# Splitting and reordering the first loads, and a tile transposed by DMA instead of TensorE

## The chip, the cores and the metric

The kernel runs on one core of one Trainium2 chip. A core has a matmul engine (TensorE, PE in the profile), VectorE (DVE), ScalarE (ACT), GpSimd (POOL) and SyncE (SP), which run their own instruction lists and wait for each other by semaphores. SP and ACT can issue DMAs, each on a queue of its own; 16 DMA engines carry them. The metric is the device time of one execution in microseconds (us). Before the change it is 214.48 us, the median of 3 runs (214.37 to 214.8).

## The reference

From x (2048 x 512, bfloat16) it computes x + attention(layernorm(x)) + FFN(layernorm(x)).

```python
xn = _layernorm(x, axis=-1)
return x + _A_ref(xn, A_wqkv, A_wo) + _B_ref(xn, B_w_gate, B_w_up, B_w_down)
# _A_ref: linear attention, H = 32 heads of Dh = 16
phi = lambda t: jnp.where(t > 0, t + 1, jnp.exp(t)) + 1e-6
pq, pk = phi(q), phi(k)
kv = jnp.einsum("bhsd,bhse->bhde", pk, v)
z = jnp.einsum("bhsd->bhd", pk)
num = jnp.einsum("bhqd,bhde->bhqe", pq, kv)
den = jnp.einsum("bhqd,bhd->bhq", pq, z)[..., None] + 1e-6
# o = num / den, times wo
# _B_ref: (silu(x @ w_gate) * (x @ w_up)) @ w_down, F = 1792
```

## The kernel before

The 2048 rows of x are 16 tiles of 128 rows. Row p*16 + t of x is partition p of tile t, so a load of one tile moves 128 pieces of 1 KB, and a load of n tiles 128 pieces of n KB.

**Stage 1** goes over the tiles. For each tile, DVE computes the mean and variance (`bns` and `agg`, lines 273 and 276), POOL the reciprocal root (`rstd_pow`, lines 292 and 299), and DVE the normalized tile xn (line 281). xn is then transposed into xnT, since a projection needs the transpose as its stationary operand. Tiles 0 to 2 are transposed by PE against an identity matrix, and ACT copies the result out of PSUM (`transpose_half` for tile 0 in two halves, lines 336 and 345; `transpose_pe` for tiles 1 and 2, lines 308 and 315). From tile 3 on the DMA engines transpose, issued by SP (`transpose_dma`, line 352). PE projects K and Q of the tile, four matmuls each (`proj`, line 361; tile 0's K in two halves, line 374). ACT computes the exponentials of K and Q and a copy of Q (lines 397, 403, 407), DVE turns K into pk (`feat_k`: a clip at line 414 and a max-add at line 423). POOL adds pk up (line 448). PE then adds xn.T @ pk over all tiles in four PSUM banks, four matmuls per tile (`gtacc`, line 456, "GT" below). V is never projected: GT times wv gives the attention's kv later.

**Stage 2** is the FFN (line 548 for gate and up projections, in chunks of 512 rows) with the attention's small products between its matmuls, and the output tiles (lines 681 and 691), which DVE adds to x and SP stores.

What sets the order is the program text: each engine runs its instructions in the order in which the functions are called, and `_Prog` adds the semaphore waits. Around the change that is:
- Loads. SP issues x 0, the first half of wk, x 2, the first half of wq, then x 4-5 (which wait for x 0 and x 1 by the `after` list of `xload`), x 6-9, x 10-11 and x 12-15. ACT issues x 1, the second half of wk, x 3 and the second half of wq. Line 192 is the x load, line 199 the weight load.
- Idle matmuls. `fill` (line 244) multiplies a tile of zeros ahead of the first real work on PE: ten at once, one behind the variance of tile 0, one behind its reciprocal root, and one between tile 0's transposes and K.
- DVE's order at the start: stats 0, stats 1, xn 0 in halves, xn 1, stats 2, stats 3, xn 2, pk 0, xn 3.
- PE's order at the start: idle matmuls, transposes 0, K 0, transposes 1, Q 0, transposes 2, K 1, Q 1. In the loop over t (lines 505 to 531) K and Q of tile t follow for t >= 2, then GT of tile t - 2.
- SP has the x loads first in its list, then the transposes as they are called, then the FFN's weights (`wpiece` at line 210 in tiles 2, 4, 6 and 8, the rest from tile 11 on).

Of the kernel before, what the change touches and what calls it, by code (L numbers as in the profile page):

```python
# [10 lines left out]
P = 128  # L11
# [97 lines left out]
def bass_parallel_sum__linear_attn_block__swiglu_ffn__prompt_kernel(  # L109
# [12 lines left out]
    K = _Prog()  # L122
    pe, act, dve, pool, sp = nc.tensor, nc.scalar, nc.vector, nc.gpsimd, nc.sync
    bf, f32 = dt.bfloat16, dt.float32

    with contextlib.ExitStack() as es:
        E = es.enter_context

        def sb(name, shape, d=bf):
            return E(nc.sbuf_tensor(name, [P] + shape, d))  # L130

        x_sb = sb("x_sb", [NT, D])
# [11 lines left out]
        stats = sb("stats", [NT, 6], f32)  # L144
        mv = sb("mv", [NT, 2], f32)
        vpe = sb("vpe", [NT], f32)
        rstd = sb("rstd", [NT], f32)
# [35 lines left out]
        def bk(i):  # L183
            return ("bank", i)


        xv = xin.rearrange("(p t) d -> p t d", t=NT)
        ov = oview.rearrange("(p t) d -> p t d", t=NT)

        def xload(eng, h, t0, n, after=()):  # L190
            K.dma(
                eng, lambda: h.dma_start(x_sb[:, t0:t0 + n, :], xv[:, t0:t0 + n, :]),  # L192
                r=list(after), w=[("x", t0 + i) for i in range(n)],
            )

        def wqkv_load(eng, h, name, i, c0, n):
            K.dma(
                eng,
                lambda: h.dma_start(  # L199
                    wqkv_sb[:, c0:c0 + n, i * D:(i + 1) * D],  # L200
                    A_wqkv[c0 * P:(c0 + n) * P, i * D:(i + 1) * D].rearrange("(c p) f -> p c f", p=P),
                ),
                w=[(name, c0)],
            )
# [4 lines left out]
        def wpiece(name, dst, src, c):  # L209
            K.dma("sp", lambda: sp.dma_start(dst[:, c, :], src[c * P:(c + 1) * P, :]), w=[(name, c)])  # L210

        xload("sp", sp, 0, 1)
        xload("act", act, 1, 1)
        wqkv_load("sp", sp, "wk", 1, 0, 2)
        wqkv_load("act", act, "wk", 1, 2, 2)
        xload("sp", sp, 2, 1)
        xload("act", act, 3, 1)
        wqkv_load("sp", sp, "wq", 0, 0, 2)
        wqkv_load("act", act, "wq", 0, 2, 2)
        xload("sp", sp, 4, 2, [("x", 0), ("x", 1)])  # L220
        xload("sp", sp, 6, 4)
        xload("sp", sp, 10, 2)
        xload("sp", sp, 12, 4)

# [10 lines left out]
            r=[("ident",)], w=[("ident",)],  # L235
# [4 lines left out]
        def fill(n, after):  # L240
            K.op(
                "pe",
                [
                    (lambda: pe.matmul(banks[3], idle[:, 0:P], idle[:, :], start=True, stop=True))
                    for _ in range(n)
                ],
                r=[("idle",)] + after, w=[bk(3)],
            )
# [21 lines left out]


        def bns(t):
            K.op("dve", lambda: dve.bn_stats(stats[:, t, :], x_sb[:, t, :]), r=[("x", t)], w=[("st", t)])  # L273

        def agg(t):
            K.op("dve", lambda: dve.bn_aggr(mv[:, t, :], stats[:, t, :]), r=[("st", t)], w=[("mv", t)])

        def xn_dve(t):
            K.op(
                "dve",  # L280
                lambda: dve.tensor_scalar(
                    out=xn_sb[:, t, :], in0=x_sb[:, t, :], scalar1=mv[:, t, 0:1], scalar2=rstd[:, t:t + 1],
                    op0=ALU.subtract, op1=ALU.mult,
                ),
                r=[("x", t), ("mv", t), ("rstd", t)], w=[("xn", t)],
            )

        def rstd_pow(t):
            eng, h = ("dve", dve) if t == 0 else ("pool", pool)
            K.op(  # L290
                eng,
                lambda: h.tensor_scalar(
                    out=vpe[:, t:t + 1], in0=mv[:, t, 1:2], scalar1=1e-5, scalar2=None, op0=ALU.add,
                ),
                r=[("mv", t)], w=[("vpe", t)],
            )
            K.op(
                "pool",
                lambda: pool.tensor_tensor(out=rstd[:, t:t + 1], in0=vpe[:, t:t + 1], in1=nhalf[:, :], op=ALU.pow),
                r=[("vpe", t), ("nhalf",)], w=[("rstd", t)],  # L300
            )

        def transpose_pe(t, b):
            tb = banks[b].bitcast(bf)[:, 0:512].rearrange("p (c s) -> p c s", c=NDC)
            K.op(
                "pe",
                [
                    (lambda c=c: pe.transpose(tb[:, c, :], xn_sb[:, t, c * P:(c + 1) * P], ident[:, :]))  # L308
                    for c in range(NDC)
                ],  # L310
                r=[("xn", t), ("ident",)], w=[bk(b)],
            )
            K.op(
                "act",
                lambda: act.activation(xnT[:, :, t * P:(t + 1) * P], tb, ACT.Copy),
                r=[bk(b)], w=[("xnT", t)],
            )
# [31 lines left out]
        def transpose_dma(t):  # L349
            K.dma(  # L350
                "sp",
                lambda: sp.dma_start_transpose(out=xnT[:, :, t * P:(t + 1) * P], in_=xn_sb[:, t, :]),
                r=[("xn", t)], w=[("xnT", t)],
            )
# [15 lines left out]
        def proj_half(t, b, lo, wname, h):  # L370
            K.op(
                "pe",
                [
                    (lambda c=c: pe.matmul(
                        banks[b], xnT[:, c, t * P:(t + 1) * P], wqkv_sb[:, c, lo:lo + D],
                        start=(c == 0), stop=(c == NDC - 1),
                    ))
                    for c in (2 * h, 2 * h + 1)
                ],
                r=[("xnTh", t, h), (wname, 2 * h)], w=[bk(b)],  # L380
            )

        def kb(t):
            return 2 * (t % 2)
# [4 lines left out]
        def kproj(t):  # L389
            proj(t, kb(t), D, "wk")  # L390

        def qproj(t):
            proj(t, qb(t), 0, "wq")

        def exp_k(t):
            K.op(
                "act", lambda: act.activation(ek[:, t % NE, :], banks[kb(t)], ACT.Exp),  # L397
                r=[bk(kb(t))], w=[("ek", t % NE)],
            )
# [52 lines left out]
        def gtacc(t):  # L452
            K.op(
                "pe",
                [
                    (lambda c=c: pe.matmul(  # L456
                        banks[4 + c], xn_sb[:, t, c * P:(c + 1) * P], pkq[:, t, 0, :],
                        start=(t == 0), stop=(t == NT - 1),
                    ))
                    for c in range(NDC)  # L460
                ],
                r=[("xn", t), ("pk", t)], w=[bk(4 + c) for c in range(NDC)],
            )

        def stat(t):
            bns(t)
            agg(t)
            rstd_pow(t)

        def xn(t):  # L470
            xn_dve(t)
            if t >= 3:
                transpose_dma(t)

        stat(0)
        stat(1)
        xn_half(0, 0)
        xn_half(0, 1)
        xn_dve(1)
        stat(2)  # L480
        stat(3)
        xn_dve(2)

        fill(10, [])
        fill(1, [("mv", 0)])
        fill(1, [("rstd", 0)])
        transpose_half(0, 4, 0)
        transpose_half(0, 5, 1)
        fill(1, [])
        proj_half(0, kb(0), D, "wk", 0)  # L490
        proj_half(0, kb(0), D, "wk", 1)
        exp_k(0)
        transpose_pe(1, 6)
        qproj(0)
        exp_q(0)
        transpose_pe(2, 7)
        kproj(1)
        qproj(1)
        feat_k(0)
        xn(3)  # L500

        STAT = {0: (4, 5), 1: (6,), 2: (7,), 3: (8,), 4: (9, 10), 5: (11,), 6: (12,), 7: (13,), 8: (14, 15)}
        XN = {0: (4,), 1: (5,), 2: (6,), 3: (7,), 4: (8,), 5: (9, 10), 6: (11,), 7: (12,), 8: (13,), 9: (14, 15)}

        for t in range(NT):
            if t >= 2:
                kproj(t)
            if t >= 1:
                exp_k(t)
            if t >= 2:  # L510
                qproj(t)
            if t >= 1:
                exp_q(t)
                feat_k(t)
            for i in STAT.get(t, ()):
                stat(i)
            for i in XN.get(t, ()):
                xn(i)
            if t in (2, 4, 6, 8):
                wpiece("wg", wg_sb, B_w_gate, t // 2 - 1)  # L520
            if t == 11:
                for c in range(NDC):
                    wpiece("wu", wu_sb, B_w_up, c)
                wqkv_load("sp", sp, "wv", 2, 0, 4)
                wload("sp", sp, "wo", wo_sb, A_wo)
            if t == 14:
                wload("sp", sp, "wd", wd_sb, B_w_down)
            if t == 12:
                masks()
            if t >= 2:  # L530
                gtacc(t - 2)
        zsum(NT - 1, None)
        gtacc(NT - 2)
# [247 lines left out]
```

## Time and profile before

| what | us |
|---|---|
| median of 3 runs | 214.48 |
| the profiled execution | 215.03 |
| its span, first to last instruction | 213.8 |
| PE busy in the span | 208.2 (97%) |
| DVE, ACT, POOL busy | 117.9, 68.0, 70.1 |
| x 0 issued, statistics of tile 0 begin | 0.80, 3.94 |
| first transposes on PE | 6.34 |
| second half of wq issued on ACT, lands | 2.27, 9.36 |
| Q of tile 0 begins | 9.50 |
| first DMA transpose (tile 3) issued | 10.86 |
| first GT (tile 0) begins | 14.25 |

In a line of the timeline the columns are start, length (us), engine, line of the kernel, operation, the tile that is written and those that are read, shapes, and the count of instructions that were merged; in brackets stands the idle time before it and what ended it. SPq and ACTq are the queues' issuing instructions; PEld is PE's load of a stationary operand. Matmul ends are modelled (379 ns each); the distance from one to the next is their pace. In a line of DMA issues the last number is the time from issue to landing.

### The profile page before, as it was taken

How to read it: one execution, taken by the hardware profiler on the slowest of the kernel's cores; microseconds unless marked ns; L12 is line 12 of the kernel's file. 1: busy time of each engine (PE TensorE's matmuls, PEld its weight loads, DVE VectorE, ACT ScalarE, POOL GpSimd, SP SyncE). 2: the span in 40 equal slices, each digit the busy share in tenths (PEclk: the TensorE clock that was granted, in tenths of full speed). 3: DMA queues.
4: the chain of work that ended last, by engine and by line, in shares of the span. 5: the costliest groups of instructions: out<-in, count | busy, mean ns of one | idle time of the engine just before them, and what ended most of it. 6: DMA issues, size and time to landing. Idle time of an engine off the chain costs nothing.

```text
span 213.8 us, 2737 instructions
## 1 busy us (share of the span) xinstructions
PE 208.2 (97%) x974; PEld 96.2 (45%) x993; DVE 117.9 (55%) x239; ACT 68.0 (32%) x118; POOL 70.1 (33%) x93
## 2 busy tenths in 40 slices
PE   7799999999999999999999999999999999999996
PEld 2344444444544444444444444444444444444455
DVE  2899987333667777345463647365467364232121
ACT  2386666667463332213031303122132213121000
POOL 1559886647044444241212422141224140000000
PEclk9999999999999999999999999999999999999999
DMA  6925697898000111110111110101101102000001
GB/s 186 385 67 132 147 143 173 286 367 259 0 15 9 28 26 31 41 25 28 26 37 37 25 28 25 49 0 49 28 25 25 49 0 52 13 11 28 25 28 51
DMA packets 24495, 15.79 MB, mean 74 GB/s; under 512 B 16416, under 2 KB 22944, under 8 KB 24480
## 3 DMA queue, kind: packets, MB, share of 16 engines
q1 hardware_dynamic: 23648, 14.82, 26.6%
q10 hardware_dynamic: 832, 0.79, 1.1%
q8 instruction: 8, 0.13, 0.3%
q14 instruction: 7, 0.06, 0.1%
HBM read 9.70 MB, written 2.10 MB: 55 GB/s over the span
## 4 chain that ended last, share of the span: by engine, by line
PE 94%; DMA 3%; ACTq 1%; issue 1%; DVE 0%
PE psum L548 45%; PE psum L691 23%; PE psum L361 13%; PE psum L681 6%; PE psum L456 6%; DMA wqkv_sb<-in_A_wqkv_dram 3%; ACTq L192 0%; PE psum L607 0%; PE psum L630 0%; ACTq L199 0%; DVE out_sb L704 0%; PE psum L597 0%; PE psum L308 0%
## 5 line engine op out<-in xcount | busy, mean ns | idle before, releaser
L563 ACT ACTIVATE sg<-psum 128x512 bf16<-128x512 f32 x56 | 33.4, 598 | 105.4 <-PE psum L548 104.6
L548 PE MATMUL psum<-xnT,wg_sb 128*128 128x512 bf16 x224 | 57.5, 379 | 0.0
L548 PE MATMUL psum<-xnT,wu_sb 128*128 128x512 bf16 x215 | 56.7, 379 | 0.5
L639 POOL TENSOR_TENSOR prod<-pkq,zb 128x512 f32<-128x512 bf16 x16 | 18.6, 1162 | 51.5 <-DVE pkq L423 51.5
L548 PEld LDWEIGHTS psum<-xnT,wu_sb 128*128 128x128 bf16 x224 | 21.9, 98 | 26.4
L548 PEld LDWEIGHTS psum<-xnT,wg_sb 128*128 128x128 bf16 x224 | 21.9, 98 | 26.4
L704 DVE TENSOR_TENSOR out_sb<-psum,x_sb 128x512 bf16<-128x512 f32 (+1 forms) x17 | 11.2, 660 | 40.9 <-PE psum L691 40.9
L361 PE MATMUL psum<-wqkv_sb,xnT 128*128 128x512 bf16 x122 | 28.9, 379 | 1.3 <-DMA wqkv_sb<-in_A_wqkv_dram 1.1
L569 DVE TENSOR_TENSOR xn_sb<-psum,sg 128x512 bf16<-128x512 f32 x28 | 19.0, 680 | 18.7 <-PE psum L548 18.2
L663 POOL TENSOR_TENSOR pqn<-pkq,rden 128x512 bf16<-128x512 bf16 x16 | 16.9, 1055 | 36.6 <-DVE rden L657 36.6
L691 PE MATMUL psum<-wd_sb,xn_sb 128*128 128x512 bf16 (+1 forms) x124 | 25.6, 355 | 0.1
L691 PE MATMUL psum<-wd_sb,pkq 128*128 128x512 bf16 x109 | 25.3, 379 | 0.2
L569 DVE TENSOR_TENSOR pkq<-psum,sg 128x512 bf16<-128x512 f32 x28 | 18.8, 673 | 11.3 <-PE psum L548 8.5
L448 POOL TENSOR_TENSOR zacc<-zacc,pkq 128x512 f32<-128x512 f32 x15 | 17.3, 1154 | 6.9 <-DVE ek L414 6.7
L361 PEld LDWEIGHTS psum<-wqkv_sb,xnT 128*128 128x128 bf16 x124 | 11.9, 98 | 15.5 <-issue 1.3
L691 PEld LDWEIGHTS psum<-wd_sb,xn_sb 128*128 128x128 bf16 x126 | 12.2, 98 | 12.1 <-DVE xn_sb L569 0.5
L691 PEld LDWEIGHTS psum<-wd_sb,pkq 128*128 128x128 bf16 x112 | 11.0, 98 | 13.2
L681 PE MATMUL psum<-m_sb,eq 128*128 128x512 bf16 (+1 forms) x68 | 16.6, 366 | 0.0
L456 PE MATMUL psum<-pkq,xn_sb 128*128 128x512 bf16 x62 | 15.8, 379 | 0.1
L647 DVE TENSOR_REDUCE den<-prod 128x32 f32<-128x512 f32 x16 | 10.9, 683 | 5.8 <-POOL prod L639 5.8
L397 ACT ACTIVATE ek<-psum 128x512 bf16<-128x512 f32 x16 | 9.6, 599 | 9.9 <-issue 3.5
L273 DVE BATCH_NORM_STATS2 stats<-x_sb 128x6 f32<-128x512 bf16 x16 | 10.8, 678 | 2.8 <-DMA x_sb<-in_A_x_dram 2.8
(57 smaller groups left out, 126.3 us busy)
## 6 DMA issues: line engine op xcount, KB each, us to landing
out_dram<-out_sb SPq DMA_DIRECT2D x15, 128.0 KB, 1.7
wg_sb<-in_B_w_gate_dram SPq DMA_DIRECT2D x4, 448.0 KB, 4.2
wu_sb<-in_B_w_up_dram SPq DMA_DIRECT2D x4, 448.0 KB, 4.7
wd_sb<-in_B_w_down_dram SPq DMA_DIRECT2D x1, 1792.0 KB, 13.5
x_sb<-in_A_x_dram SPq DMA_DIRECT2D x2, 512.0 KB, 5.9
wqkv_sb<-in_A_wqkv_dram ACTq DMA_DIRECT2D x2, 256.0 KB, 5.7
wqkv_sb<-in_A_wqkv_dram SPq DMA_DIRECT2D x2, 256.0 KB, 4.7
x_sb<-in_A_x_dram SPq DMA_DIRECT2D x2, 256.0 KB, 5.1
```

Source lines behind the costliest of these rows:

```text
L361: (lambda c=c: pe.matmul(banks[b], xnT[:, c, t * P:(t + 1) * P], wqkv_sb[:, c, lo:lo + D], start=(c == 0), stop=(c == NDC - 1),))
L448: lambda: pool.tensor_tensor(out=zacc[:, :], in0=zacc[:, :], in1=pk, op=ALU.add),
L456: (lambda c=c: pe.matmul(banks[4 + c], xn_sb[:, t, c * P:(c + 1) * P], pkq[:, t, 0, :], start=(t == 0), stop=(t == NT - 1),))
L548: (lambda c=c: pe.matmul(banks[b], w_sb[:, c, fc * P:(fc + 1) * P], xnT[:, c, C * 512:(C + 1) * 512], start=(c == 0), stop=(c == NDC - 1),))
L563: lambda: act.activation(sg[:, j % NSG, :], banks[gb], ACT.Silu),
L569: lambda: dve.tensor_tensor(out=hT(C, fc), in0=banks[ub], in1=sg[:, j % NSG, :], op=ALU.mult,),
L639: lambda: pool.tensor_tensor(out=p, in0=pkq[:, t, 1, :], in1=zb[:, :], op=ALU.mult),
L647: lambda: dve.tensor_reduce(out=d, in_=p.rearrange("p (h e) -> p h e", e=DH), op=ALU.add, axis=AX.X,),
L663: lambda: pool.tensor_tensor(out=pqn[:, t % NPN, :].rearrange("p (h e) -> p h e", e=DH), in0=pkq[:, t, 1, :].rearrange("p (h e) -> p h e", ...
L681: (lambda g=g: pe.matmul(dst, pqnT(t)[:, g, :], m_sb[:, g, lo:hi], start=(g == 0), stop=False,))
L691: (lambda fc=fc: pe.matmul(dst, hT(C, fc)[:, jj * P:(jj + 1) * P], wd_sb[:, fc, lo:hi], start=False, stop=(fc == NFC - 1),))
L704: lambda: dve.tensor_tensor(out=o, in0=src, in1=x_sb[:, t, lo:hi], op=ALU.add),
```

## The change

x 0 is loaded in two parts of 64 rows, one on each queue. x 2 moves ahead of the weights on SP; x 3 moves from ACT to SP, behind wq; x 4-5 wait for both halves of wk, x 6-9 for both halves of wq, and x 10 to 15 follow. Tile 2 is transposed by DMA. DVE takes stats 2 ahead of xn 1 and stats 3 ahead of xn 2. On PE, three of the idle matmuls go, transposes 1 stand ahead of exp of K 0 in ACT's list too, and GT of tile 0 is called ahead of the loop, so that it comes before K of tile 2. In the loop, tiles 2 to 4 are followed by GT of tile t - 1, tile 5 by none, and later tiles by GT of tile t - 2 as before.

```diff
-        xload("sp", sp, 0, 1)
+        def xpart(eng, h, t, p0):
+            K.dma(
+                eng, lambda: h.dma_start(x_sb[p0:p0 + P // 2, t, :], xv[p0:p0 + P // 2, t, :]),
+                w=[("xp", t, p0)] + ([("x", t)] if p0 else []),
+            )
+
+        wk, wq = [("wk", 0), ("wk", 2)], [("wq", 0), ("wq", 2)]
+        xpart("sp", sp, 0, 0)
+        xpart("act", act, 0, P // 2)
         xload("act", act, 1, 1)
+        xload("sp", sp, 2, 1)
         wqkv_load("sp", sp, "wk", 1, 0, 2)
         wqkv_load("act", act, "wk", 1, 2, 2)
-        xload("sp", sp, 2, 1)
-        xload("act", act, 3, 1)
         wqkv_load("sp", sp, "wq", 0, 0, 2)
         wqkv_load("act", act, "wq", 0, 2, 2)
-        xload("sp", sp, 4, 2, [("x", 0), ("x", 1)])
-        xload("sp", sp, 6, 4)
+        xload("sp", sp, 3, 1)
+        xload("sp", sp, 4, 2, wk)
+        xload("sp", sp, 6, 4, wq)
         xload("sp", sp, 10, 2)
         xload("sp", sp, 12, 4)
...
         def bns(t):
-            K.op("dve", lambda: dve.bn_stats(stats[:, t, :], x_sb[:, t, :]), r=[("x", t)], w=[("st", t)])
+            K.op("dve", lambda: dve.bn_stats(stats[:, t, :], x_sb[:, t, :]),
+                 r=[("x", t)] + ([("xp", t, 0)] if t == 0 else []), w=[("st", t)])
...
         def xn(t):
             xn_dve(t)
-            if t >= 3:
+            if t >= 2:
                 transpose_dma(t)
...
         xn_half(0, 0)
         xn_half(0, 1)
-        xn_dve(1)
         stat(2)
+        xn(1)
         stat(3)
-        xn_dve(2)
+        xn(2)
 
         fill(10, [])
-        fill(1, [("mv", 0)])
-        fill(1, [("rstd", 0)])
         transpose_half(0, 4, 0)
         transpose_half(0, 5, 1)
-        fill(1, [])
         proj_half(0, kb(0), D, "wk", 0)
         proj_half(0, kb(0), D, "wk", 1)
+        transpose_pe(1, 6)
         exp_k(0)
-        transpose_pe(1, 6)
         qproj(0)
         exp_q(0)
-        transpose_pe(2, 7)
         kproj(1)
         qproj(1)
         feat_k(0)
         xn(3)
-
+        gtacc(0)
+
+        SKIP = 5
...
-            if t >= 2:
+            if 2 <= t < SKIP:
+                gtacc(t - 1)
+            elif t > SKIP:
                 gtacc(t - 2)
```

## The prediction

> **What bounds the kernel now.** I first read the busy shares, then the chain that ended last, then the first 18 us in order of time, and last how long single DMAs take to land. From the page:
>
> ```profile
> span 213.8 us, 2737 instructions
> ...
> PE 208.2 (97%) x974; PEld 96.2 (45%) x993; DVE 117.9 (55%) x239; ACT 68.0 (32%) x118; POOL 70.1 (33%) x93
> ...
> PE 94%; DMA 3%; ACTq 1%; issue 1%; DVE 0%
> ```
>
> PE is the engine that sets the end; the one other thing in the chain is 3% of DMA. The chain in order of time says where it lies (start, length, what):
>
> ```profile
> 2.27 7.09 DMA wqkv_sb<-in_A_wqkv_dram
> 9.50 1.02 PE psum L361 x4
> 10.75 3.45 PE psum L361 x16
> 14.25 0.81 PE psum L456 x3
> 15.06 1.73 PE psum L361 x8
> ```
>
> The second half of wq, issued on ACT's queue at 2.27, lands at 9.36, Q of tile 0 waits for it, and from 9.50 PE runs without a hole worth naming to the end. At 15.11 (14.25 and four matmuls of 0.216) it has done K and Q of tiles 0, 1, 2 and GT of tile 0. After the change the same work lies behind it when Q of tile 2 ends, since GT of tile 0 now comes ahead of K of tile 2. So the whole question is **when Q of tile 2 ends: before 15.11 is a gain, after it a loss**, one for one, if nothing stalls later. The rows that the new start hangs on, from the timeline:
>
> ```profile
> 1.25 5.25 PE L244 MATMUL psum<-idle 128*128 128x512 bf16 x12 [1.25 <-DVE idle L238]
> ...
> 3.94 0.69 DVE L273 BATCH_NORM_STATS2 stats<-x_sb 128x6 f32<-128x512 bf16 x1 [2.75 <-DMA x_sb<-in_A_x_dram]
> ...
> 4.18 1.91 SPq L192 DMA_DIRECT2D x_sb<-in_A_x_dram  x4
> ...
> 9.18 0.41 DVE L281 TENSOR_SCALAR xn_sb<-x_sb,mv,rstd 128x512 bf16<-128x512 bf16 x1 [0.20 <-POOL rstd L299]
> ...
> 10.86 7.62 SPq L352 DMA_TRANSPOSE xnT<-xn_sb  x4
> ```
>
> The reader sees: the idle matmuls begin at 1.25 on an otherwise empty PE, x 0 sets when DVE begins, xn 2 is written at 9.18, and SP issues x 4 to 15 already at 4.18 to 6.09, long before the first DMA transpose at 10.86, so the transposes never meet the x loads. And from the DMA view, single issues (KB, us to landing): the transpose issued at 17.30, the first piece of w_gate at 18.53, and the transpose behind that piece on SP's queue at 19.46:
>
> ```profile
> xnT<-xn_sb SPq DMA_TRANSPOSE x1, 2.4
> ...
> wg_sb<-in_B_w_gate_dram SPq DMA_DIRECT2D x1, 448.0 KB, 3.8
> ...
> xnT<-xn_sb SPq DMA_TRANSPOSE x1, 3.4
> ```
>
> A transpose with nothing ahead of it takes 2.4 us, one with a load ahead of it on SP's queue lands 0.59 us after that load (22.89 against 22.30). A queue serves in order.
>
> **The change, part by part.**
>
> Ten idle matmuls instead of thirteen. The three that go are 0.43, 0.43 and 0.22 us on PE. The ten end at 1.25 + 10 x 0.427 = 5.52, and PE idles until xn of tile 0 is there. Fills are 0.43 apart until 6.1, K of tile 0 is 0.22 apart from 7.09, though the granted clock reads 1.00 throughout: PE doubles its pace at about 6.3. If the hole of some 0.4 us at 5.5 keeps the pace low for a few us more, the two halves of K 0, four transposes and about three matmuls of Q 0 cost 0.86 + 0.2 + 0.65 = 1.7 us more. I cost it at nothing: the wait for tile 2 (below) covers it. The page "TensorE: Matmul & The Clock Gate" of the Trainium skill (section "What's actually happening") says that the pace follows how busy PE has lately been, and that about 3.4 us of busy time release it, so by it a thinner warm-up is a risk and not a saving. Put into the sum, its bad case moves the end of GT 0 from 11.4 to about 12.9, still short of the landing found below, and the time stays.
>
> x 0 in two halves. Both queues start with 64 rows; one more DMA issue, of 0.3 to 0.4 us, lands on each queue's front. x 0 landed at 3.92 (0.80 + 3.1) with x 1 beside it at 4.10. Bounds: nothing, to 0.5 us earlier; I take 0.2, so x 0 at 3.7; the first transposes on PE stand at 6.34 now. The chain DVE (stats 0, stats 1, two halves), PE, ACT then runs 0.2 earlier, and the fills that held the transposes to 6.34 are gone: transposes at 5.95, K 0 done at 7.6 instead of 7.97.
>
> xn 1 behind stats 2. Costs 0.69 + 0.18 on DVE, but xn 1 had waited 0.60 for rstd: xn 1 ends about 7.4 as now. Its PE transposes stand at 7.6, the ACT copy (0.6) at 7.9 to 8.5, now ahead of exp of K 0 (done 9.0); clip and max-add of tile 0 end at about 10.1.
>
> Order of loads. In both kernels x 0 to 3, wk and wq are 1,536 KB in rows of 1 KB. Only x 3 moves behind wq, and x 4 to 15 leave wq alone. SP's own half of wq landed at 7.6 (2.22 + 5.4); ACT's half was the one that dragged to 9.36 beside the large x packets. Bounds for both halves: 7.3 (7.6 less x 3's 128 KB at 0.35 KB/ns, and that rate is 16 packets of 1 KB in 46 ns) to 8.4 (ACT's half drags for half as long as now). I take 7.8. wk has x 2 ahead of it now and comes 0.4 us later than 5.5, still ahead of K 0's 6.7. x 3 lands with wq at about 7.8; stats 3 (0.69 + 0.18) follow, and xn 2, queued behind them, ends at about 9.2 against 9.59 now.
>
> PE's chain: Q 0 from 7.9, K 1, Q 1, GT 0, sixteen matmuls at 0.216 = 3.45: it ends at 11.4. pk of tile 0 (10.1) and wq are there in time. Four PE transposes of tile 2 (0.22) and one ACT copy (0.6) are gone.
>
> Tile 2 by DMA transpose, **the step that decides**. In SP's order ahead of it stand x 4 to 5, which wait for wk, and x 6 to 15 (1,280 KB), which wait for both halves of wq. So SP issues x 6 to 15 from 7.85 to about 9.1, then the transpose (xn 2 is there) at about 9.2. Alone it would land at 11.6. But it stands on SP's queue behind 1,280 KB whose first byte can't come before about 8.9 (issue to first packet is 1.0 us for w_gate's piece). When x 12 to 15 land:
> - lower bound 12.5: the shortest load-like issue on the page (128 KB of output, 1.7 us), and the other 1,152 KB at the rate of x 6 to 15 now (1,280 KB between the landings of x 4-5 at 8.65 and x 12-15 at 11.92: 0.39 KB/ns, 2.95 us): 7.85 + 1.7 + 2.95.
> - upper bound 13.8: w_gate's 448 KB in 3.8 us, and 832 KB at the same rate in 2.13: 7.85 + 3.8 + 2.13.
> I take 13.1, the middle: w_gate's piece began from an idle DMA system, and here the pause is short. The page "DMA: Bandwidth & Descriptors" (section "Anatomy of one DMA") gives 2.0 us and the bytes at 436 GB/s for the other issuing path; an estimate by it is 7.85 + 2.0 + 3.0 = 12.85, and the final sum by it would be 214.65.
> The transpose lands 0.59 later, by the row of 19.46: 13.7. K 2 starts 0.1 behind that, 13.8.
>
> What queues behind that wait: K 2, Q 2, GT 1 and all of PE. Tile 3's transpose is behind tile 2's on SP (1.19 us of issue each) and lands about 0.6 to 0.9 later, 14.6; K 3 needs it at 16.4. pk of tile 1 (DVE: stats 4 and 5, xn 4, clip, max-add after 10.5) is there at about 13.8; GT 1 needs it at 15.5. These don't stall. GT one tile earlier in tiles 2 to 4 and the skip at tile 5 add no matmul.
>
> **Sum.** PE stands still from 11.4 to 13.8, K 2 and Q 2 take 8 x 0.216 = 1.73, Q 2 ends at 15.53, against 15.11: **0.4 us slower**. What the change wins at Q 0 (1.6 us), the transpose waits away, and a little more. The profiled execution took 215.03 us around its span of 213.8; it would be 215.45. It stands 0.55 above the median of 214.48, and I put the difference on the median: **214.9**.
>
> With both bounds: wq at 7.3 and x 12-15 at their lower bound give K 2 at 12.7 and 0.7 us gained; wq at 8.4 and the upper bound 15.1 and 1.7 us lost; wq at 7.8 alone gives 0.2 gained to 1.1 lost. A change within 0.2% (0.43 us) is about what a measurement of this kernel can't tell from none.
>
> **Rivals.**
> 1. The wait for tile 2 comes out just as long as the gain (within 0.43 us; wq at 7.4 to 7.8 with loads near the middle). For it: the bounds straddle zero. 214.5.
> 2. The loads run quicker: wq lands by 7.4 and x 6 to 15 stream without a start-up pause, K 2 at about 12.7. For it: with x 4 to 15 away, wq has the DMA engines to itself. Against it: one DMA engine's share of wq dragged, and SP waits for the last. 213.8.
> 3. The other side, by one mechanism: the transpose doesn't stand behind the x loads. It then lands 2.4 us after 9.2, K 2 starts at 11.7 and Q 2 ends at 13.4; GT 1 waits for pk 1 until 13.8: 1.3 to 1.4 us gained, 213.1. It turns to a gain as soon as K 2 starts before 13.38. For it: PE is free by 11.4. Against it: the 3.4 against 2.4 us.
> 4. The pace of PE drops in the hole of 2.4 us before K 2. Some 3.4 us at half pace cost 1.7: 216.6. Against it: the hole of 1.15 us at 8.35 now costs no pace (0.216 from 9.50 on).
> 5. The reordering doesn't do what it says: wq lands at 9.36 as now, and x 6 to 15, which wait for it, move 1.56 later than in the sum: 216.5. For it: the straggling engine may lag from the start. Against it: what it shared its time with, the large x packets, is gone.
>
> **How the numbers follow.** Slower by the queued transpose 0.42, rivals 4 and 5 0.04 each: slower 0.50. Rival 1: 0.27. Rival 2 0.12 and rival 3 0.11: faster 0.23. The likeliest case's own range is 214.5 to 215.7. The range for 8 in 10 leaves out rivals 3, 4 and 5, 0.19 together: 213.6 to 215.9.
>
> **What the changed profile would show.** Right: Q 0 at about 7.9 with no wait of 1 us for wq; a hole on PE of about 2 us ahead of the third K, ended by the transpose's DMA; SP's transpose of tile 2 issued at about 9.2 with more than 4 us to landing; x 12 to 15 landing at about 13; PE without holes from 16 on. Wrong: the third K starting at 11 to 12 (the queue doesn't hold it), matmuls 0.43 apart behind 6.3, or a hole at K 3 or GT 1, which would mean that DVE is late.

## The result and the profile after

The changed kernel takes 220.73 us (median of 6 runs, 219.65 to 221.36) against 214.52 us (median of 6 runs, 214.37 to 215.08): a ratio of 1.0281, 95% interval 1.026 to 1.0301. The profiled execution took 220.03 us with a span of 218.7, 4.9 more than the span before. The medians are 6.2 apart, 1.2 more than the two profiled executions, since the one before lies 0.5 above its median and the one after 0.7 below; what follows explains the profiled difference. From the page:

```profile
span 218.7 us, 2726 instructions
...
PE 208.8 (95%) x967; PEld 95.8 (44%) x986; DVE 118.0 (54%) x239; ACT 67.5 (31%) x117; POOL 70.1 (32%) x93
...
PE 91%; DMA 5%; DVE 1%; SPq 1%; issue 1%; DVEq 0%
```

PE's busy time is nearly the same (208.8 us against 208.2); what was added is time in which PE had nothing to do or did it slowly. The chain in order of time says where (start, length, what):

```profile
3.03 5.32 DMA x_sb<-in_A_x_dram
...
8.37 0.70 DVE stats L281
...
9.60 6.01 DMA xnT<-xn_sb
...
15.75 3.50 PE psum L370 x8
```

The chain no longer goes through wq. It goes through x 3 (issued at 3.03, landed at 8.34), its statistics, which stand ahead of xn 2 on DVE, tile 2's transpose on SP's queue, issued at 9.60 and landed 6.0 us later, and then eight matmuls, K 2 and Q 2, that take 3.50 us instead of 1.89. PE's own rows around it, from the timeline of PE:

```profile
8.19 2.75 PE L370 MATMUL psum<-wqkv_sb,xnT 128*128 128x512 bf16 x12
10.78 1.03 PE L465 MATMUL psum<-pkq,xn_sb 128*128 128x512 bf16 x4
15.75 3.50 PE L370 MATMUL psum<-wqkv_sb,xnT 128*128 128x512 bf16 x8 [3.95 <-DMA xnT<-xn_sb]
```

Q 0 starts at 8.19, 1.3 us earlier than in the profile before, GT 0 is done at 11.65 (10.78 and four steps of 0.216), and then PE waits until 15.75, 4.1 us; the bracket says 3.95 because it counts from the modelled end of the last matmul. Single loads and the transpose in the DMA view (KB, us to landing): x 6 to 9 issued at 8.12, x 10 and 11 at 8.5, x 12 to 15 at 8.97, the transpose at 9.60:

```profile
x_sb<-in_A_x_dram SPq DMA_DIRECT2D x1, 512.0 KB, 4.3
...
x_sb<-in_A_x_dram SPq DMA_DIRECT2D x1, 256.0 KB, 5.0
...
x_sb<-in_A_x_dram SPq DMA_DIRECT2D x1, 512.0 KB, 6.1
...
xnT<-xn_sb SPq DMA_TRANSPOSE x1, 6.0
```

The last x load lands at 15.04 and the transpose at 15.62, 0.58 behind it. Last, busy time and granted clock by stretch (us, then busy us and instructions of PE, PEld, DVE, ACT, POOL, then PEclk, DMA share, GB/s):

```profile
12.00:15.00 3.00, 0.00 (x0) 0.00 (x0) 2.69 (x8) 0.07 (x1) 2.01 (x5) 1.00 1.05 239
16.00:19.00 3.00, 3.00 (x8) 1.03 (x7) 0.68 (x2) 0.60 (x1) 0.34 (x1) 0.50 0.23 44
20.00:24.00 4.00, 4.00 (x19) 1.82 (x19) 2.48 (x7) 2.40 (x5) 2.30 (x4) 1.00 0.43 87
```

While PE is empty the DMA engines are full (share 1.05) and yet move only 239 GB/s. That is the pace of the x loads as a whole: from their first packet at 9.09 to the end of their last at 14.66 they moved 1,280 KB, 235 GB/s. Behind the hole PE runs at a granted clock of 0.50, for 3.41 us by the record, and then at 1.00 again.

The sum over the profiled execution: GT 0 behind K 0 to 2 and Q 0 to 2 was done at 14.90 before; the same work is done at 19.09 now, 4.19 later. A second, short wait of 0.34 at K of tile 9 (34.63 to 34.97; its transpose landed at 34.88) brings FFN's start from 50.30 to 54.83, 4.53 later:

```profile
34.97 1.89 PE L370 MATMUL psum<-wqkv_sb,xnT 128*128 128x512 bf16 x8 [0.18 <-issue]
```

The last 0.4 lies in the FFN; 0.21 of it is a wait for DVE at 201.35, and the rest stays open. Four of the six executions had a mean granted clock of 0.991 or 0.992 and two of 0.984 (spans of 220.0), which is one or two stretches of 3.4 us at half pace; that explains a part of the spread from 219.65 to 221.36.

### The profile page after: what moved, and what is told of

Same layout as the page of the kernel before. It is cut to its first block, busy times and chain, and to the rows that moved or that the text cites. A ratio compares the mean times of both kernels' runs of the same rounds, so it can differ in the third digit from the quotient of the medians.

```text
span 218.7 us, 2726 instructions
## 1 busy us (share of the span) xinstructions
PE 208.8 (95%) x967; PEld 95.8 (44%) x986; DVE 118.0 (54%) x239; ACT 67.5 (31%) x117; POOL 70.1 (32%) x93
## 4 chain that ended last, share of the span: by engine, by line
PE 91%; DMA 5%; DVE 1%; SPq 1%; issue 1%; DVEq 0%
PE psum L557 44%; PE psum L700 22%; PE psum L370 12%; PE psum L690 6%; PE psum L465 6%; DMA xnT<-xn_sb 3%; DMA x_sb<-in_A_x_dram 2%; PE psum L616 0%; SPq L199 0%; PE psum L639 0%; DVE stats L281 0%; DVE xn_sb L578 0%; SPq L214 0%; SPq L192 0%; DVE out_sb L713 0%
## 5 line engine op out<-in xcount | busy, mean ns | idle before, releaser
L370 PE MATMUL psum<-wqkv_sb,xnT 128*128 128x512 bf16 x122 | 30.4, 394 | 4.2 <-DMA xnT<-xn_sb 3.9
## 6 DMA issues: line engine op xcount, KB each, us to landing
wd_sb<-in_B_w_down_dram SPq DMA_DIRECT2D x1, 1792.0 KB, 12.4
```

Of the source, the lines that this page charges most:

```text
L370: (lambda c=c: pe.matmul(banks[b], xnT[:, c, t * P:(t + 1) * P], wqkv_sb[:, c, lo:lo + D], start=(c == 0), stop=(c == NDC - 1),))
```

## The experiments

Where nothing else is said, the edit is made to the changed kernel ("after"). Every time is a median, and the ratio with its interval is to the kernel before, on the same chip; it is taken from all the runs and is not the ratio of two medians.

**e1: idle matmuls in the hole.**

```diff
         gtacc(0)
+        fillb(16, 0)
```

`fillb(n, b)`, added for this run, puts n idle matmuls into PSUM bank b.

> The changed kernel with sixteen more idle matmuls behind GT of tile 0, in the PSUM bank that K of tile 2 overwrites, so that PE is busy through most of the hole of 3.9 us ahead of K 2 (11.65 to 15.1). Everything else stays. Theory 'pace' (the hole itself halves PE's pace for 3.4 us): K 2 and Q 2 are 0.216 apart and take 1.7 us instead of 3.4, the transpose still lands at about 15.6, and the time falls by about 1.6 us or a little more, to about 219.0. Rival (the slow K 2 and Q 2 come from something else, such as reading what the DMA has just written): K 2 and Q 2 still take 3.3 and the time stays at 220.7.

Measured: 219.03 us, ratio 1.0191 (1.0166 to 1.0216), 1.7 us less than after (1.9 by the two ratios). PE's timeline:

```profile
13.36 3.62 PE L262 MATMUL psum<-idle 128*128 128x512 bf16 x16
16.81 1.89 PE L380 MATMUL psum<-wqkv_sb,xnT 128*128 128x512 bf16 x8
```

K 2 and Q 2 are at full pace again, although they read the same freshly transposed tile: the hole itself had halved the pace. In this execution the pace was already lost once, at 7.32 to 10.73, behind 3.41 us in which PE had been busy for 1.70, so that the fills ran late and pushed K 2 0.4 behind its transpose (landed at 16.44); the 1.6 us of the hole's price came back all the same.

**e2: tile 2 on PE again.**

```diff
-            if t >= 2:
+            if t >= 3:
                 transpose_dma(t)
...
         exp_q(0)
+        transpose_pe(2, 7)
         kproj(1)
```

> The changed kernel with tile 2 transposed on PE again (behind Q 0, as before the change); loads, the ten idle matmuls and GT 0 ahead of K 2 stay. Theory 'queue and pace' (all of the loss is the wait for tile 2's transpose behind x 6 to 15, and the slow pace after it): no hole ahead of K 2, no slow matmuls, Q 0 still at about 8.2 instead of 9.5, so about 1.2 us faster than before the change: 213.3. Rival (the reordered loads themselves do the harm, x 6 to 15 arriving late for DVE): a hole later in stage 1 and a time of 215 or more.

Measured: 215.96 us, ratio 1.0052 (1.0033 to 1.0071). The large loss is gone, so it does hang on tile 2's transpose, but the expected gain isn't there. In the profiled execution the full pace came only at 10.1 us, and K 0 took 1.89 us instead of 1.04; Q 0 started at 9.49.

**e3: the transpose ahead of the loads.**

```diff
-        xload("sp", sp, 6, 4, wq)
-        xload("sp", sp, 10, 2)
-        xload("sp", sp, 12, 4)
...
         xn(2)
+        xload("sp", sp, 6, 4, wq)
+        xload("sp", sp, 10, 2)
+        xload("sp", sp, 12, 4)
```

> The changed kernel with x 6 to 15 called behind xn of tile 2, so that SP issues tile 2's transpose first and these loads after it. Theory 'queue' (a transpose waits for what stands ahead of it on SP's queue): tile 2's transpose lands 2.4 to 2.6 us after its issue at about 9.6, K 2 starts at about 12.2; the wait moves to tile 3, whose transpose now stands behind x 6 to 15 and takes 6 us or more. The time is not better than 218. Rival 'contention' (the transpose is slow because the DMA engines are full with loads, wherever it stands): tile 2's transpose still takes well over 3 us, because x 6 to 15 begin to move 1 us after it.

Measured: 220.72 us (one execution). Tile 2's transpose, issued at 10.02, landed at 12.54, 2.5 us later. The wait went to tile 3, whose transpose now stood behind the loads (the first line is K 2 and Q 2, the second K 3 and Q 3):

```profile
12.68 1.89 PE L367 MATMUL psum<-wqkv_sb,xnT 128*128 128x512 bf16 x8 [0.36 <-ACT pkq L413]
...
19.22 3.03 PE L367 MATMUL psum<-wqkv_sb,xnT 128*128 128x512 bf16 x8 [3.64 <-DMA xnT<-xn_sb]
```

The same transpose takes 2.5 us ahead of the loads and 6.0 behind them, and tile 3's, behind them now, 6.1 (issued 12.94, landed 19.08). The loads were issued at 11.43 and hardly moved yet while tile 2's transpose did, so this run doesn't exclude contention. Nor does e11, where the transpose takes 2.5 us too: its packets begin at 11.0, when the last x packets start. That the order on SP's queue decides is shown; whether full DMA engines would also hold a transpose that stands ahead of the loads, or on the other queue, is not tested.

**e4: x 4 to 15 without waits on the weights.**

```diff
-        xload("sp", sp, 4, 2, wk)
-        xload("sp", sp, 6, 4, wq)
+        xload("sp", sp, 4, 2, [("x", 0), ("x", 1)])
+        xload("sp", sp, 6, 4)
```

> The changed kernel with x 4 to 15 waiting for x 0 and x 1 alone, as before the change, so that they are issued from about 3.5 us on. Theory 'queue': the loads are over by about 11.5 to 12, tile 2's transpose at 9.6 stands behind a short rest of them and lands at about 12.2 to 12.8, K 2 starts there, and the time is within 0.5 us of before, 214.0 to 214.8. Rival (the wait of the loads doesn't matter, x 6 to 15 are slow in any order beside the transposes): the transpose lands at 14 or later and the time stays above 218.

Measured: 216.11 us, ratio 1.0063 (1.0037 to 1.009). Neither theory's numbers. Two of the sixteen DMA engines were late with their share of wk, which came at 8.53; K 0 started at 8.67, and PE, which had waited 1.94 us for wk, ran at a granted clock of 0.50 from 9.90 to 13.32 and reached the end of GT 0 only at 14.9, behind the transpose (issued 10.99, landed 14.24). This execution, at 218.37 us, was the slowest of the twelve and is not typical. So most of the loss goes with the waits of the loads, but this run doesn't separate why.

**e5: no second wait on SP.**

```diff
-        xload("sp", sp, 6, 4, wq)
+        xload("sp", sp, 6, 4)
```

> The changed kernel with x 6 to 15 no longer waiting for wq: they follow x 4-5 at once, behind the wait for wk (from about 6.6 us). Theory 'restart' (x 6 to 15 took 6.9 us from issue to the last landing because the DMA engines had run empty before them, and would stream 1,280 KB in 3.3 us behind other loads): x 12 to 15 land at about 12.0 to 12.7, tile 2's transpose at 12.6 to 13.3, K 2 starts there, a hole of about 1.5 us is left and PE keeps its pace; the time is 216 to 217.5. Rival (these loads are slow whenever the weights have gone first): x 12 to 15 still land behind 14 and the time stays above 219.

Measured: 219.01 us, ratio 1.0187 (1.0162 to 1.0212). By its numbers the rival's, but the edit failed at its purpose: three DMA engines were late with wk (8.22), x 4 to 15 waited for it, and the queue ran empty in this version as well before they began. PE waited 1.76 us for wk and then ran at half pace from 8.15 to 11.57. In the trace the slow part is the start of the stream: ten reads of x 4-5 took 0.6 to 0.9 us for 2 KB, and the 1,280 KB behind them took 3.45 us from the landing of x 4-5 (11.55) to that of x 12-15 (15.00), against 5.60 in after (9.44 to 15.04). That fits a slow restart, but the time alone would not tell.

**e6: tile 2 on PE and thirteen idle matmuls** (e2's edit, and the three fills back).

```diff
         fill(10, [])
+        fill(1, [("mv", 0)])
+        fill(1, [("rstd", 0)])
         transpose_half(0, 4, 0)
         transpose_half(0, 5, 1)
+        fill(1, [])
```

> The changed kernel with tile 2 transposed on PE and the three idle matmuls back where they were; of the change only the loads, the order of DVE and GT 0 ahead of K 2 are left. Theory 'warm-up' (with ten idle matmuls PE starts K 0, Q 0 and K 1 at half pace in most executions, which cost the version with tile 2 on PE its gain): K 0 is 0.22 apart, Q 0 starts at about 8.3, K 2 at about 11.7, and the time is 213.0 to 213.6. Rival (the version with tile 2 on PE was slow for another reason, such as the loads): the time stays at 215 to 216.

Measured: 216.55 us, ratio 1.0072 (1.0044 to 1.0101): a miss. The warm-up was right (K 0 in 1.04 us, Q 0 at 8.57), but K 2 started at 12.89 and not at 11.7, 0.47 of it a wait for xn 2, and then PE waited for tile 3:

```profile
16.43 1.89 PE L370 MATMUL psum<-wqkv_sb,xnT 128*128 128x512 bf16 x8 [0.79 <-DMA xnT<-xn_sb]
```

Tile 3's transpose, now the first on SP's queue, stands behind x 12 to 15 (landed 15.75) and lands at 16.30. The order of the loads hurts whichever tile comes first; moving tile 2 back to PE only hands the wait on. K of tile 9 waited another 0.98.

**e7: the kernel before with ten idle matmuls.**

```diff
-        fill(1, [("mv", 0)])
-        fill(1, [("rstd", 0)])
...
-        fill(1, [])
```

> The kernel before the change with ten idle matmuls instead of thirteen and nothing else changed. Theory 'warm-up': PE is idle from about 5.5 to 6.0, the full pace comes a window of 3.4 us later in most executions, K 0 and the transposes run at half pace, but Q 0 waits for wq until 9.4 anyway; so the price is what is left behind 9.5 at half pace: 0 to 1.5 us, median 215.0 to 216.0. Rival (the idle matmuls do nothing): 214.5, and a gain of up to 0.2.

Measured: 215.02 us, ratio 1.0 (0.9981 to 1.002). Full pace came at 10.3 in the profile, and K 0 went at half pace:

```profile
7.27 1.89 PE L374 MATMUL psum<-wqkv_sb,xnT 128*128 128x512 bf16 x4 [0.22 <-ACT xnT L345]
```

K 0 cost 0.85 more and four matmuls of Q 0 started at 9.38; GT 0 was done at 15.2 instead of 14.9. Nothing hides that here: wq had landed at 8.37, ahead of Q 0, and in the profile of e14, with thirteen idle matmuls, GT 0 is done at 14.35. Why the ratio is 1.0 all the same isn't shown.

**e8: after with thirteen idle matmuls** (e6's fills alone).

> The changed kernel with the three idle matmuls back. Prediction's step (the thinner warm-up is covered by the wait for tile 2's transpose): K 2 starts with the transpose's landing at about 15.7 as before this edit, the hole and the slow K 2 and Q 2 stay, and the time is that of the changed kernel, 220 to 221. Rival (the warm-up is part of the loss): 219 or less.

Measured: 220.64 us, ratio 1.0268 (1.0241 to 1.0295), as after. K 2 started at 16.24, with a hole of 4.1 us ahead of it, and took 3.53 with Q 2. The warm-up is no part of the loss.

**e9: loads without a pause** (with the fills of e6).

```diff
-        xload("sp", sp, 4, 2, wk)
-        xload("sp", sp, 6, 4, wq)
+        xload("sp", sp, 4, 2, [("x", 2)])
+        xload("sp", sp, 6, 4)
```

> The changed kernel with the three idle matmuls back, and x 4 to 15 waiting for x 2 alone (it lands at about 4.9), so that they are issued from 5 us on and their descriptors stand on SP's queue before wq is through. Theory 'restart' (x 6 to 15 were slow because the queue had run empty ahead of them): loads run on without a pause, x 12 to 15 land at about 12, tile 2's transpose at 12.3 to 12.8, K 2 starts there, Q 2 ends at 14.1 to 14.6, and the time is 213.8 to 214.6. Rival (loads of x behind the weights are slow in any case): the transpose lands behind 14 and the time is 216 or more.

Measured: 217.13 us, ratio 1.0083 (1.0055 to 1.0111), between the two theories. From the landing of x 4-5 (9.89) to that of x 12-15 (13.16) the 1,280 KB took 3.27 us, exactly as in the kernel before; after needed 5.60 between the same two landings (9.44 to 15.04), and 6.9 from issue. No read of them took longer than 0.38 us. So the restart theory holds for the loads. They ended 1.2 us later than expected, the transpose landed at 13.74, and the hole shrank to 1.0 us with no loss of pace:

```profile
13.88 1.89 PE L370 MATMUL psum<-wqkv_sb,xnT 128*128 128x512 bf16 x8 [0.97 <-DMA xnT<-xn_sb]
```

The time stays above before: FFN began at 51.86, 1.56 later, with this hole and one of 0.71 at K of tile 9.

**e10: e9 with tile 2 on PE** (e2's edit added).

> As the run with x 4 to 15 waiting for x 2 and thirteen idle matmuls, and with tile 2 transposed on PE. Theory 'queue': no transpose stands behind a long rest of loads, tile 3's transpose lands at about 13.5, well before K 3; Q 0 starts at about 8.5, nothing stalls, and the time is 213.3 to 214.0, faster than before. Rival (loads of x behind the weights are slow in any case): tile 3's transpose lands behind 15.5, K 3 waits, and the time is 215.5 or more.

Measured: 215.91 us, ratio 1.0035 (1.0012 to 1.0057). As theory 'queue' said, tile 3's transpose landed at 13.84 and nothing waited for it. The gain was small (tile 2's transposes, ahead of K 1, waited 0.54 for xn 2, which waits for x 3's statistics), and it was lost at tile 9:

```profile
31.12 1.89 PE L370 MATMUL psum<-wqkv_sb,xnT 128*128 128x512 bf16 x8 [0.83 <-ACT pkq L416]
```

ACT had long been done; tile 9's transpose landed at 31.03. It was issued at 24.98 behind a piece of w_gate (issued 24.02, landed 28.98) on SP's queue. But it landed 2.05 us behind that piece, where those behind the other pieces came 0.54 to 0.59 behind theirs; with 0.6 it would have been there before K of tile 9 was due (30.29). The queue alone doesn't make this wait.

**e11: the kernel before with tile 2 by DMA.** Loads and idle matmuls as before; of the change only the transpose and the order of GT.

```diff
-            if t >= 3:
+            if t >= 2:
                 transpose_dma(t)
...
-        transpose_pe(2, 7)
...
+        gtacc(0)
...
-            if t >= 2:
+            if 2 <= t < SKIP:
+                gtacc(t - 1)
+            elif t > SKIP:
                 gtacc(t - 2)
```

> The kernel before the change with tile 2 by DMA transpose, GT 0 ahead of K 2 and the order of GT in tiles 2 to 5 as in the change; loads and the thirteen idle matmuls as before. Theory 'queue': the x loads are through by 11.9, the transpose at about 9.7 waits for their rest and lands at 12.3 to 12.8, when PE is at the end of GT 0 (about 12.9); so no hole, and a gain of about 0.2 us: 214.2 to 214.6. Rival (the DMA transpose of tile 2 costs by itself, whatever the loads do): a hole of 1 us or more ahead of K 2 and 215.5 or more.

Measured: 215.62 us, ratio 1.003 (1.0013 to 1.0047). The transpose landed at 12.29, 0.57 behind x 12-15, as the queue says, K 2 started at 12.34 with next to no hole, and in the profiled execution (214.72 us) stage 1 ended 0.7 us earlier than before. The median is nevertheless 0.3% worse than before; the profiled execution is the fastest of twelve and doesn't show why. Alone, this part costs some 0.6 us, not 6.

**e12: the kernel before with x 3 behind wq.**

```diff
-        xload("act", act, 3, 1)
...
         wqkv_load("act", act, "wq", 0, 2, 2)
+        xload("sp", sp, 3, 1)
```

> The kernel before the change with x 3 moved from ACT's queue, ahead of wq, to SP's queue behind wq; nothing else. The second half of wq has 128 KB less ahead of it on ACT's queue and lands 0.4 to 1.5 us earlier than 9.36; the loads go on without a pause. Theory (PE's start waits for wq): Q 0 starts at 8.4 to 9.1 and the time falls by 0.4 to 1.0 us, to 213.5 to 214.1. Rival (the one engine that drags decides, wherever x 3 stands): 214.5.

Measured: 214.92 us, ratio 1.0 (0.9988 to 1.0013). Q 0 started at 8.28, but tile 2's transposes, which stand ahead of K 1, then waited 0.61 us for xn 2. FFN began 0.43 earlier than in the profile before, and the time is the same. The profile of e14, with x 3 where it was, has the same start, so no gain from this move is shown:

```profile
8.16 1.03 PE L361 MATMUL psum<-wqkv_sb,xnT 128*128 128x512 bf16 x4
9.80 0.40 PE L308 MATMUL psum<-ident,xn_sb 128*128 128x128 bf16 x4 [0.61 <-DVE xn_sb L281]
```

**e13 and e14: w_gate behind the transposes**, in e10 and in the kernel before.

```diff
-            if t in (2, 4, 6, 8):
-                wpiece("wg", wg_sb, B_w_gate, t // 2 - 1)
+            if t == 9:
+                for c in range(NDC):
+                    wpiece("wg", wg_sb, B_w_gate, c)
```

> The version with x 4 to 15 waiting for x 2, thirteen idle matmuls and tile 2 transposed on PE, with the four pieces of w_gate called in tile 9, behind the last transpose, instead of in tiles 2, 4, 6 and 8. Theory 'queue' (the wait of about 1 us at tile 9 is its transpose standing behind a piece of w_gate on SP's queue): no wait at tile 9, FFN begins at about 50.0 instead of 50.97, and the time falls by 0.8 to 1.0 us, to about 215.0. Rival (the wait at tile 9 comes from DVE or from the DMA engines as such): FFN still begins at 50.9 and the time stays at 215.9.

> The kernel before the change with the four pieces of w_gate called in tile 9; nothing else. Theory 'queue': PE waited for no transpose in the kernel before, so its time stays, 214.4 to 215.0. Rival (the later w_gate and with it w_up come too late for FFN at 50.3): a hole at FFN's start and 215.5 or more.

Measured: e13 214.98 us, ratio 1.0003 (0.9988 to 1.0017), 0.9 below e10 (0.7 by the ratios), with no wait at tile 9 and FFN at 49.90. So moving w_gate takes the wait away, though something else holds transposes too: with no load ahead of them on SP's queue, those issued at 26.09 and 27.40 took 4.25 and 3.64 us instead of 2.4, early enough for PE not to wait. What it is stays open. e14 214.47 us, ratio 0.9981 (0.9967 to 0.9995): better than the kernel before by 0.2%, which was not expected. In the twelve runs of e14 all times lie between 214.35 and 214.86, while the kernel before had 35 runs between 214.34 and 215.69. That the longer of these wait at tile 9 too is likely, but it isn't shown: the profile before is of one that doesn't, by 0.09 us (its tile 9's transpose landed at 30.35, and K starts at 30.45).

**e15 and e16: the parts together**, on the kernel before: e12's loads, the order of GT, tile 2's PE transposes behind Q 1, and w_gate late (e15) or as before (e16).

```diff
         exp_q(0)
-        transpose_pe(2, 7)
         kproj(1)
         qproj(1)
+        transpose_pe(2, 1)
...
+        gtacc(0)
```

> The kernel before the change with x 3 behind wq on SP, tile 2's PE transposes behind Q 1 (in bank 1) and GT 0 ahead of K 2, the order of GT in tiles 2 to 5 as in the change, and the pieces of w_gate in tile 9. Thirteen idle matmuls. Theory: Q 0 at 8.3 to 8.5, no wait for xn 2 ahead of K 1, Q 2 ends at 13.7 to 14.0 instead of 14.9, no wait at tile 9, and the time is 0.7 to 1.2 us below before: 213.3 to 213.9. Rival (what is won at the start is lost again to another wait in stage 1): 214.5 or more.

> As the run that puts the parts together, with the pieces of w_gate in tiles 2, 4, 6 and 8 as before the change. Theory 'queue': Q 2 ends as early, but PE meets tile 9's transpose behind w_gate and waits 0.3 to 1 us there, so the time is 0.3 to 0.9 us above that run. Rival: no difference.

Measured: e15 214.88 us, ratio 0.9999 (0.9985 to 1.0013); e16 215.45 us, ratio 1.0021 (1.0003 to 1.0039). The difference of 0.6 is w_gate's place again: e16 waits 0.80 at tile 9, whose transpose landed 2.06 behind the piece of w_gate (FFN at 50.48), and e15 doesn't (49.92). But the hoped-for gain went: GT 1 now stands ahead of K 3 and waited for pk 1 on DVE (0.21 us), and K 2 followed at 12.4 only. PE's order alone doesn't win the start here, since DVE sets pk 1. Of all versions e14 is the fastest.

## Why the prediction was wrong

**The direction and the place were right.** K 2 waits for tile 2's transpose, which waits behind x 6 to 15 on SP's queue; Q 0's gain was 1.3 us (forecast 1.6), and it was all waited away. e3 shows that the order on the queue decides (2.5 us ahead of the loads, 6.0 behind them), and in e6 tile 3's transpose, now the first behind the loads, waits in the same way. The small terms held: wq at 8.06 (7.8 was taken, 8.4 the bound), GT 0 done at 11.65 (11.4), the transpose issued at 9.60 (9.2), 0.58 us from the last load to the transpose (0.59; the profile before has a row of 2.05 as well, from 28.30 to 30.35, which was not used).

**The term that failed is "When x 12 to 15 land".** It was put between 12.5 and 13.8 and taken at 13.1; they landed at 15.04. The rate of 0.39 KB/ns was read from loads whose predecessors were still moving, and the longest start-up was that of 448 KB of w_gate. Of the 1.9 us that this step was short, 0.3 is wq's later landing. The rest is that x 6 to 15, which started on a queue run empty, moved at 235 GB/s and not at 390: from the landing of x 4-5 to that of x 12-15 they took 5.60 us. e4, e9 and e10, with the pause removed and the same loads, have the old 3.2 to 3.3 us. Why a restarted stream is slow is open: thirteen of its 256 reads of 4 KB took 0.6 to 1.3 us instead of 0.16, and none did so in the kernel before.

The page of the Trainium skill that the forecast weighed, "DMA: Bandwidth & Descriptors" (section "Anatomy of one DMA"), has a fit for the other issuing path, by which an estimate is 5.0 us from the wait's end; 6.9 us were measured from issue, and the measurement decides.

**Rival 4 happened, and the argument against it was too weak.** Its price was right: 1.7 us forecast, 1.6 measured (GT 1 follows K 2's start by 3.34 us instead of 1.73; the steps are 0.427 instead of 0.216). It got a chance of 0.04 because a hole of 1.15 us had cost no pace. With the landing 1.9 us later the hole grew from 2.4 to 4.1 us, and the 3.41 us ahead of the drop (the record has it at 15.64) held no matmul at all; e1 shows that the hole is the cause. But a shorter hole can be enough. The record of the clock changes in steps of 3.41 us. Once PE was at full pace, half pace followed each step in which it had been busy for half of the time or less (0 in after and e8, 0.17 in e3, 0.32 in e5, 0.43 in e4, 0.50 in e1), the longest hole 1.5 to 1.9 us in e1, e4 and e5, and none with 0.59 or more (0.59 at the end of e5, 0.62 in the kernel before around its 1.15 us, 0.72 in e9 around its 1.0 us). With K 2 at 13.8, as forecast, the share from 12.23 to 15.64 would be an estimated 0.54, between the two. So the late landing made the slow pace here, and whether the forecast hole would have made it too is open.

The page "TensorE: Matmul & The Clock Gate" ("What's actually happening") was weighed in the forecast for the warm-up alone; it also puts the half-rate state behind an idle window of about 3.4 us. The hole of 4.1 us agrees with that, and the loss in e1, e4 and e5 came with less.

**The other rivals fell.** Rivals 1 and 2 needed the loads to land by 13; rival 3, the transpose passing the loads, is refuted by the landing 0.58 behind them, and by e3 and e6; rival 5, wq as late as before, by its landing at 8.06.

**The point of comparison was off by 0.21.** GT 0 began at 14.04 and ended at 14.90, not 15.11: the timeline merged three of four matmuls, and the first record was missing. The next K (14.90) would have told.

**And wq was late in that one execution.** In the profile before, fifteen of the sixteen DMA engines had ended the second half of wq by 8.00 and one at 9.36, and that one is what Q 0 waited for. With the same loads in the same order wq landed at 7.78 in e11, 7.98 in e14 and 8.37 in e7, and in e14 Q 0 starts at 8.16, as in the changed kernel (8.19). So the 1.3 us at Q 0 are won against one late engine, and in e14's execution there was nothing to win. The large x packets beside wq, which the forecast took for the reason, were there in these three too.

**"The transposes never meet the x loads" was wrong in time.** Tile 3's transpose before was issued at 10.86, and x 12 to 15 landed at 11.92; it took 2.50 us all the same.

**"Ten idle matmuls ... I cost it at nothing" was right for the changed kernel.** e8 puts the three back and the time stays; e7 takes them from the kernel before, and the time stays there as well, though K 0 goes at half pace. (The bad case adds 1.7 to 11.4, which is 13.1 and not 12.9; it stays short of the landing.)

**"PE without holes from 16 on" was wrong by 0.34.** The forecast looked for w_gate's piece only as a row to read the queue from, and not as the next thing that a transpose would stand behind: tile 9's, issued at 29.40 behind a piece that landed at 34.35, landed at 34.88. In e13, with these pieces moved, no K waits there.

Over the sum: K 2 1.95 later than forecast, 1.6 for the pace, 0.2 for the comparison, 0.7 later on, together 4.5, to the 0.4 of the forecast: 4.9, which is the profiled difference; the 1.2 us by which the medians differ more are not traced.

## What to carry to other kernels

A transpose by DMA, or any transfer that PE waits for, can be as late as what stands ahead of it on its issuing engine's queue (0.58 us behind 1,280 KB of loads here): before one is moved, list the queue at that moment in bytes, and ask when the last of them lands. A wait that holds loads back until others are through also lets the queue run empty, and the restart can cost more than the wait gains: here wq landed at 8.06 to 8.57 in the new order with the wait (after, e1, e2, e3, e6, e8) and at 7.78 to 8.37 in the old order without it (e7, e11, e14). A hole on PE has two prices, its length and the half pace that can follow it, here behind every 3.41 us in which PE was busy for half of the time or less. And one late engine in one profiled execution is not a property of the kernel: look at a second execution before the order is rebuilt around it.

## What the runs showed of the hardware that was not expected

- A stream of loads that starts on an empty queue was slow, with the DMA engines shown as busy: the 1,280 KB of x 6 to 15 took 4.7 to 5.9 us between the landings of x 4-5 and x 12-15 behind the pause (after, e1, e2, e6, e8), and 3.2 to 3.4 in eleven profiles of a running stream. In e5, where the pause lay ahead of x 4-5, they took 3.45.
- The granted clock dropped to 0.50 for 3.41 us right behind a hole of 4.1 us, and came back by itself with PE busy. It dropped as well behind 3.41 us in which PE had been busy for 0.32 (e5), 0.43 (e4) and 0.50 (e1), and not behind 0.59 (e5, at its end) and 0.62 (the kernel before).
- A warm-up of ten idle matmuls reached full pace at 5.4 us in the profile of after, and at 10.1 and 10.3 us in those of e2 and e7: the same ten can be enough or not.
- In after the sixteen completions of x 12 to 15, which a transpose follows on the queue, came within 0.1 us of each other (14.94 to 15.04), while those of x 10 and 11 were spread over 2 us (11.57 to 13.53). The same holds in e1, e3, e5, e6 and e8, but in e2, e4 and e9, where a transpose follows too, x 12 to 15 are spread over 1.4 to 1.7 us.
- In the profiles before, of e10 and of e16 the transpose behind the second piece of w_gate landed 2.05 us behind it instead of 0.5 to 0.8 as behind the others; e13 has transposes of 4.25 and 3.64 us at that time with no load ahead of them.
